# Two MLPs behind an attention: stages spread, fewer loads, and one head group's q and k transposed on VectorE

## The chip, the cores and the metric

The kernel runs on one core of a Trainium2 chip. The metric is device microseconds (us) of one execution; a kernel's time is the median of its runs. Engines are named as the profile names them: PE (TensorE matmuls), PEld (its weight loads), DVE (VectorE), ACT (ScalarE), POOL (GpSimd) and SP (SyncE, which issues nearly all DMAs).

## The reference

Attention over 4 batches, 8 heads, 576 positions of 64 features. Heads 0 to 3 are local (a position sees the 32 before it), heads 4 to 7 strided (a position sees earlier ones that are congruent modulo 32). The output, 2304 tokens of 512, goes through two MLPs (hidden width 2048). The attention weights are float32; the four MLP weight matrices are float64 and are given to the kernel as their 64 bits.

```python
scores = where(mask, scale * (q @ k.T), -1e9)
attn   = softmax(scores)
x = (attn @ v).transpose(0, 2, 1, 3).reshape(2304, 512)
h = x @ w_in;  g = h * clip(h + 3, 0, 6) / 6;          x = g @ w_out      # first MLP
h = x @ w_in2; g = max(h, 0) + log1p(exp(-abs(h)));    out = g @ w_out2   # second MLP
```

## The kernel before

**Tiling.** Layer `l` = 0 is the first MLP, `l` = 1 the second. A layer runs over token chunks `c` and, inside a chunk, over 16 steps `f` of 128 hidden features. Layer 0 has five chunks: `c` = 0 with 384 tokens (the first 96 positions of all four batches) and then one batch per chunk, 480 tokens each. Layer 1 has chunks of 384 and 4 times 512. Every product is made in three passes on a high and a low half of both operands (xh/xl, wih/wil, gh/gl, woh/wol), so step `f` is 12 matmuls into `psh` (`pe_h`, L619) and 12 (layer 1: 9 or 12) into the four banks of `psy` (`pe_y`, L677), the latter two steps late: `psy` of `f` is issued after `psh` of `f` + 2. `psh` has two banks, so `psh` of `f` + 2 waits until the activation of `f` has been read out of its bank.

**The activation** (`post1`): ACT reads `psh` into `r` (L633; in layer 1 three passes, L638 to L640), DVE forms the product (`r` L634, in layer 1 L641) and with that frees the bank. `post2a` casts `r` to `gh` on ACT (L648), `post2b` forms `gl` on DVE (L654).

**Weights.** A tile of 128x512 float64 words (512 KB) is loaded by SP into one of four buffers with the tag `w64` (`load_win` L94, `load_wout` L99). `w_scale` (ACT, L110) and `w_bits` (DVE, L115 and L126) turn it into float32 in place (for w_out into `wor`), and `split_win` (ACT L137, DVE L138) and `split_wout` (ACT L144, DVE L145) make the two halves. A `w64` buffer is free once its last reader on DVE or ACT is through. In chunk 0 of layer 0 one w_in tile and one w_out tile are prepared per step `f`; layer 1's w_in tiles are prepared during the last chunk of layer 0, its w_out tiles during its own chunk 0.

**Attention.** A prologue computes the first 96 positions of every batch. The other 480 positions of batch `b` are worked in slots, two per step, during chunk `c` = `b` of layer 0, and are the input of chunk `b` + 1: stage 0 the strided heads, stage 1 the local ones. `s_load` fetches the strided heads' q, k and v for each of two head pairs (`sq`, `sk`, `vs`); `s_trans` transposes q and k on PE (18 transposes of a batch into `psq`, L462) and copies them out on ACT (`qT`, `kT`, 6 copies, L472). Then scores on PE (`pss`, L489), maximum on DVE (L509), exponentials on ACT (`sc`, L524), `psp` (transposes of the weights, L540), copied by ACT to `pt` (L546), `pso` (times v, L560), division on DVE (`xn`, L570) and `psx` (L586), which becomes xh/xl (L159 and L160). The table at the end of the builder says in which slot each piece is put.

**What sets the order.** The code is written in a framework that fixes each engine's order when the program is built; each engine then works through its list in that order, and an instruction that waits holds all that stand behind it on its engine. `after(...)` makes the pieces in its body be ordered behind a marked instruction ("DVE" is the last `r` of layer 0, "PE" the last matmul of `pe_h`). SP's list holds the DMA issues.

Of the kernel before, what the change touches and what calls it, by code (L numbers as in the profile page):

```python
# [16 lines left out]
P = 128  # L17
# [5 lines left out]
def attn_two_mlps(  # L23
# [68 lines left out]
    def load_win(l, f):  # L92
        t = wsl.tile([P, DM], I64, tag="w64", name="wi64", bufs=4)
        nc.sync.dma_start(out=t, in_=w_in[l][f].rearrange("p k f -> p (k f)"))  # L94
        wst_t[0, l, f] = t

    def load_wout(l, f):
        t = wsl.tile([P, DM], I64, tag="w64", name="wo64", bufs=4)
        nc.sync.dma_start(out=t, in_=w_out[l][f * P : (f + 1) * P, :])  # L99
        wst_t[1, l, f] = t  # L100
# [168 lines left out]
    def loc_c(bp, e):  # L269
        s = loc[bp]["s", e][0]  # L270
        ps = ps_att("psc")
        for i in range(2 * NP):
            nc.tensor.transpose(ps[:KW, i * QB : (i + 1) * QB], s[:, i], ident[:QB, :QB])
        if e == 0:
            loc[bp]["pts"] = ap.tile([P, NP, 512], F32, tag="pt", name="pt")
        pt = loc[bp]["pts"][:, e]
        nc.scalar.copy(pt[:KW, : 2 * NP * QB], ps[:KW, : 2 * NP * QB])
        loc[bp]["pt", e] = pt
# [120 lines left out]
    def s_load(b, pr):  # L399

        q, k = (in_tile(n) for n in ("sq", "sk"))
        rows = slice(b * STRIDE, (b + 1) * STRIDE)
        n = STRIDE // NG
        for g in range(NG):
            for e in range(2):
                nc.sync.dma_start(
                    out=q[:, g * P + e * D : g * P + (e + 1) * D],
                    in_=qs[b * STRIDE + n * g : b * STRIDE + n * (g + 1), 2 * pr + e, II - 1 :, :],
                )
        for g in range(5):  # L410
            r0, r1 = KR * g, min(KR * (g + 1), STRIDE)
            nc.sync.dma_start(
                out=k[: (r1 - r0) * NJ, g * P : (g + 1) * P].rearrange("p (h d) -> p h d", d=D),
                in_=ks[
                    2 * pr : 2 * pr + 2, b * STRIDE + r0 : b * STRIDE + r1
                ].rearrange("h r j d -> (r j) h d"),
            )
# [6 lines left out]
        un[0, b, pr] = dict(q=q, k=k, v=v)  # L424

# [10 lines left out]
    def l_load_v(b, pr):  # L436

        v = v_tile("vl")
        for e in range(2):
            v3 = v[e * D : (e + 1) * D].rearrange("k (i o d) -> k i o d", o=2, d=D)  # L440
            fs = slice((2 * pr + e) * D, (2 * pr + e + 1) * D)
            for o in range(2):
                n = SB // BL // 2 + 1 - o
                k0 = 2 * BL + o * BL
                nc.sync.dma_start(
                    out=v3[:, :n, o],
                    in_=vl[b, k0 : k0 + n * 2 * BL, fs].rearrange("(i k) d -> k i d", k=2 * BL),
                )
        un[1, b, pr]["v"] = v

    def s_trans(b, n, last=False):
# [82 lines left out]
    def a_pt(st, b):  # L534

        ps = ps_two("psp")
        pt = ap.tile([P, NP, 512], F32, tag="pt", name="pt")
# [90 lines left out]
    def post1(l, c, f):  # L628
# [30 lines left out]
    def pe_y(l, c, f):  # L659
# [8 lines left out]
        for m in range(n):  # L668
# [7 lines left out]
            for j, (a, bb) in enumerate(prods):  # L676
                nc.tensor.matmul(  # L677
                    o, lhsT=a, rhs=bb, start=(f == 0 and j == 0), stop=(f == NF - 1 and j == 2)
                )
# [51 lines left out]
    for b in range(B):  # L731
        o = 2 * NF * b + (3 if b == 0 else 0)
# [5 lines left out]
        put(o - 1, s_trans, b, "q")  # L738
        put(o, s_trans, b, "k")
        put(o + 1, s_trans, b, "k", True)  # L740
        for st, qk, exp, rec, pt, pv, px in (
            (0, 3, (5, 6, 7, 8), 9, 10, 12, 15),
            (1, 7, (10, 11, 13, 14), 16, 18, 20, 23),
        ):
            put(o + qk, a_qk, st, b)
            for pr in range(NP):
                put(o + qk + pr, a_max, st, b, pr)
            for n in range(2 * NP):
                put(o + exp[n], a_exp, st, b, *divmod(n, 2))
            put(o + rec, a_rec, st, b)  # L750
            put(o + pt, a_pt, st, b)
            put(o + pv, a_pv, st, b)
            put(o + px, a_px, st, b)

    with ExitStack():
# [113 lines left out]
        for pr in range(NP):  # L869
            s_load(0, pr)  # L870
        with after("xh", "xl"):
            w_scale(1, 0, 0)
# [6 lines left out]
        for n, (l, c, f) in enumerate(seq):  # L879
# [36 lines left out]
            if l == 1 and c == 0:  # L916
                if f == 0:
                    w_bits((0, 1, NF - 1))
                w_bits((1, 1, f))
            if c == 0:  # L920
                split_wout(l, c, f)
            if att:
                for u in fill.get(2 * (NF * c + f), []):
                    with after(*(["DVE", "PE"] if c == 0 else [])):
                        u()
# [5 lines left out]
            if last1:  # L931
                w_scale(0, 1, f)
                if f == NF - 1:
                    w_scale(1, 1, 0)
            if l == 1 and c == 0 and f + 1 < NF:
                w_scale(1, 1, f + 1)
            if att:
                for u in fill.get(2 * (NF * c + f) + 1, []):
                    with after(*(["DVE", "PE"] if c == 0 else [])):
                        u()  # L940
# [71 lines left out]
```

## Time and profile before

| | |
|---|---|
| median of 3 runs | 900.32 us (899.03 to 905.15) |
| profiled execution | 898.38 us, its span 896.2 us |
| mean granted clock | 0.986 of full speed |
| PE busy | 867.1 us (97%) |
| ACT busy | 519.2 us (58%) |
| DVE busy | 458.3 us (51%) |

Some 2.2 us of the profiled execution lie outside the span. PE is busy nearly all the time, so time can only be had where PE does less or where it waits; the other engines' shares are means over stretches that differ much, and have to be read by stretch.

### The profile page before, as it was taken

To read this page: it belongs to the slowest core of one execution; us is meant where nothing else is said; L and a number is where in the kernel's file an instruction comes from. 1 tells how busy PE (TensorE), PEld (TensorE's weight loads), DVE (VectorE), ACT (ScalarE), POOL (GpSimd) and SP (SyncE) were. 2 spreads that over 40 slices of the span, in tenths; PEclk is the share of its full clock that TensorE was granted. 3 is DMA by queue.
4 is the path that set the end of the run, shared out by engine and by line. 5 is a ranking of instruction groups with operands and counts; after the bars stand their busy time and mean duration, and the time that the engine had idled before them with its cause. 6 is when DMAs were issued, how large, how long until landed. Compare 5 with 4: busy or idle time off the path is not lost.

```text
span 896.2 us, 15445 instructions
## 1 busy us (share of the span) xinstructions
PE 867.1 (97%) x6107; PEld 747.6 (83%) x6107; DVE 458.3 (51%) x1019; ACT 519.2 (58%) x1142; POOL 7.6 (1%) x17
## 2 busy tenths in 40 slices
PE   4898899999999999999999899999999999999997
PEld 2797898888888888888888788888888888888996
DVE  6897855443544344455767664433443344334433
ACT  4687657434734375345545876655655565555664
POOL 3000000000000000000000000000000000000000
PEclk8899999999999999999999999999999999999999
DMA  8778831211331032004335620200110001000100
GB/s 241 222 237 200 277 91 45 64 28 29 91 69 27 24 103 47 2 3 125 108 95 194 223 95 15 68 1 0 36 48 1 1 0 48 1 1 9 39 1 36
DMA packets 82504, 65.92 MB, mean 74 GB/s; under 512 B 63872, under 2 KB 70912, under 8 KB 82432
## 3 DMA queue, kind: packets, MB, share of 16 engines
q1 hardware_dynamic: 81424, 64.35, 24.3%
q8 instruction: 48, 0.79, 0.4%
q10 hardware_dynamic: 1008, 0.59, 0.2%
q14 instruction: 24, 0.20, 0.1%
HBM read 55.44 MB, written 9.44 MB: 72 GB/s over the span
## 4 chain that ended last, share of the span: by engine, by line
PE 79%; DMA 9%; DVE 4%; ACT 4%; issue 2%; SPq 1%; ACTq 0%; DVEq 0%
PE psh L619 37%; PE psy L677 37%; DMA wi<-in_w_in_dram 5%; DMA wo<-in_w_out_dram 3%; ACT sc L524 1%; PE pso L560 1%; DVE wil L138 1%; PE pss L489 1%; ACT wi L110 1%; SPq L695 1%; PE psp L540 1%; PE psx L586 1%; ACT wo L110 1%; PE psq L462 1%; DMA lq<-in_ql_dram 1%
## 5 line engine op out<-in xcount | busy, mean ns | idle before, releaser
L619 PE MATMUL psh<-xh,wih 128*128 128x480 f32 (+2 forms) x640 | 238.9, 373 | 4.8 <-DVE r L641 2.5
L619 PE MATMUL psh<-xl,wih 128*128 128x480 f32 (+2 forms) x640 | 237.7, 372 | 0.0
L619 PE MATMUL psh<-xh,wil 128*128 128x480 f32 (+2 forms) x640 | 237.7, 372 | 0.0
L145 DVE TENSOR_TENSOR wol<-wor,woh 128x512 fp32r<-128x512 f32 x160 | 110.3, 690 | 72.1 <-ACT woh L144 68.7
L144 ACT CAST woh<-wor 128x512 fp32r<-128x512 f32 x160 | 99.0, 619 | 75.6 <-PE psy L677 74.1
L619 PEld LDWEIGHTS psh<-xh,wih 128*128 128x128 f32 x640 | 121.0, 189 | 23.4 <-DVE r L641 3.8
L619 PEld LDWEIGHTS psh<-xl,wih 128*128 128x128 f32 x640 | 121.0, 189 | 16.3 <-DVE xl L160 0.4
L641 DVE SCALAR_TENSOR_TENSOR r<-psh,r 128x512 f32<-128x512 f32 (+1 forms) x80 | 51.0, 638 | 161.4 <-ACT r L640 161.4
L619 PEld LDWEIGHTS psh<-xh,wil 128*128 128x128 f32 x640 | 120.9, 189 | 14.8
L654 DVE TENSOR_TENSOR gl<-r,gh 128x480 fp32r<-128x480 f32 (+2 forms) x160 | 101.5, 634 | 45.6 <-ACT gh L648 45.5
L677 PE MATMUL psy<-gl,woh 128*128 128x480 f32 (+1 forms) x320 | 119.9, 375 | 0.5 <-DVE gl L654 0.5
L677 PE MATMUL psy<-gh,wol 128*128 128x480 f32 (+1 forms) x320 | 118.5, 372 | 0.4 <-DVE wol L145 0.4
L677 PE MATMUL psy<-gh,woh 128*128 128x480 f32 (+1 forms) x320 | 118.4, 375 | 0.0
L648 ACT CAST gh<-r 128x480 fp32r<-128x480 f32 (+2 forms) x160 | 92.1, 575 | 42.7 <-DVE r L634 38.4
L677 PE MATMUL psy<-wol,gh 128*128 128x512 f32 x288 | 111.9, 391 | 0.0
L677 PE MATMUL psy<-woh,gl 128*128 128x512 f32 x288 | 111.6, 391 | 0.0
L677 PE MATMUL psy<-woh,gh 128*128 128x512 f32 x288 | 110.9, 390 | 0.0
L638 ACT ACTIVATE r<-psh 128x512 f32<-128x512 f32 (+1 forms) x80 | 44.4, 555 | 93.8 <-PE psh L619 93.6
L634 DVE SCALAR_TENSOR_TENSOR r<-r,psh 128x480 f32<-128x480 f32 (+1 forms) x80 | 50.4, 630 | 80.2 <-ACT r L633 80.1
L633 ACT ACTIVATE r<-psh 128x480 f32<-128x480 f32 (+1 forms) x80 | 44.5, 556 | 61.7 <-PE psh L619 60.3
L677 PEld LDWEIGHTS psy<-gl,woh 128*128 128x128 f32 x320 | 60.4, 189 | 9.0 <-DVE gl L654 1.3
L677 PEld LDWEIGHTS psy<-gh,wol 128*128 128x128 f32 x320 | 60.3, 189 | 8.5 <-DVE wol L145 1.1
(104 smaller groups left out, 834.6 us busy)
## 6 DMA issues: line engine op xcount, KB each, us to landing
wi<-in_w_in_dram SPq DMA_DIRECT2D x32, 512.0 KB
wo<-in_w_out_dram SPq DMA_DIRECT2D x32, 512.0 KB
out_dram<-vout SPq DMA_DIRECT2D x18, 256.0 KB
ydr<-ysb SPq DMA_DIRECT2D x80, 48.0 KB
yr<-ydr SPq DMA_DIRECT2D x16, 192.0 KB
vs<-in_vs_dram SPq DMA_DIRECT2D x16, 144.0 KB
sq<-in_qs_dram SPq DMA_DIRECT2D x64, 32.0 KB
lk<-in_kl_dram SPq DMA_DIRECT2D x8, 256.0 KB
```

Of the source, the lines that this page charges most:

```text
L110: nc.scalar.activation(out=h, in_=h, func=AF.Prelu, scale=2.0**-112, alpha=-(2.0**32))
L138: nc.vector.tensor_tensor(out=lo, in0=raw, in1=hi.bitcast(F32), op=ALU.subtract)
L144: nc.scalar.copy(hi, raw)
L145: nc.vector.tensor_tensor(out=lo, in0=raw, in1=hi.bitcast(F32), op=ALU.subtract)
L619: mark["PE"] = nc.tensor.matmul(ps[:, :n], lhsT=w[:, kt], rhs=x[:, :n], start=(kt == 0 and j == 0), stop=(kt == KT - 1 and j == 2),)
L633: nc.scalar.activation(out=r, in_=ps, func=AF.Relu, bias=3.0)
L634: mark["DVE"] = nc.vector.scalar_tensor_tensor(out=r, in0=r, scalar=6.0, in1=ps, op0=ALU.min, op1=ALU.mult)
L638: nc.scalar.activation(out=r, in_=ps, func=AF.Abs)
L641: nc.vector.scalar_tensor_tensor(out=r, in0=ps, scalar=0.0, in1=r, op0=ALU.max, op1=ALU.add)
L648: nc.scalar.copy(hi, g32_t[l, c, f])
L654: nc.vector.tensor_tensor(out=lo, in0=g32_t.pop((l, c, f)), in1=hi.bitcast(F32), op=ALU.subtract)
L677: nc.tensor.matmul(o, lhsT=a, rhs=bb, start=(f == 0 and j == 0), stop=(f == NF - 1 and j == 2))
```

## The change

- The loaded 512 KB weight tiles get five buffers in place of four.
- For batches 2 to 4 (`b` = 1 to 3) q and k of the strided heads are loaded by 4 + 4 DMAs per head pair, each 32 partitions by 16 or 18 rows of 128 bytes, in place of 8 + 5 DMAs with rows of 256 bytes; a new function `s_trans32` transposes them on DVE, four instructions a batch, and the PE transposes and ACT copies of these batches go. Batch 1 keeps the transposes on PE; its k comes in 3 DMAs per pair in place of 5.
- v of the strided heads is loaded by a function of its own (`s_load_v`), v of the local heads in 2 DMAs per pair in place of 4. SP's list goes from 379 rows to 329.
- The slots of the attention's pieces are spread: the exponentials of stage 1 lie at 14 to 20, its last piece at 28 of 32 (before: 10 to 14 and 23); q and k of batches 3 and 4 are loaded 14 slots ahead.
- In layer 1's chunk 0 the w_out tile is loaded two steps ahead in place of one, its `w_scale` is ordered behind the `gh` cast of the step, its `w_bits` behind the `r` of the step. The pieces of attention are ordered behind the last `psh` matmul in all chunks, and "PE" now marks matmuls of `pe_y` too.

```diff
     def load_win(l, f):
-        t = wsl.tile([P, DM], I64, tag="w64", name="wi64", bufs=4)
+        t = wsl.tile([P, DM], I64, tag="w64", name="wi64", bufs=5)
...
         q, k = (in_tile(n) for n in ("sq", "sk"))
...
+        else:
+            for t, w, src in ((q, NR, qs[rows, :, II - 1 :, :]), (k, NJ, ks[:, rows])):
+                for i in range(4):
+                    h, d0 = 2 * pr + i // 2, i % 2 * BL
+                    nc.sync.dma_start(
+                        out=t[i * BL : (i + 1) * BL, : w * BL].rearrange("r (j d) -> r j d", d=BL),
+                        in_=(src[:, h] if t is q else src[h])[:, :, d0 : d0 + BL],
+                    )
+        un[0, b, pr] = dict(q=q, k=k)
...
+    def s_trans32(b, n, pr):
+        u = un[0, b, pr]
+        w = NR if n == "q" else NJ
+        u[n + "T"] = st_tile(n + "T")
+        nc.vector.transpose(
+            out=u[n + "T"][:, : STRIDE * w].rearrange("p (r j) -> p j r", j=w),
+            in_=u[n][:, : STRIDE * w].rearrange("p (j r) -> p j r", r=STRIDE),
+        )
...
-            nc.vector.scalar_tensor_tensor(
+            mark["DVE2"] = nc.vector.scalar_tensor_tensor(
                 out=r, in0=ps, scalar=0.0, in1=r, op0=ALU.max, op1=ALU.add
             )
...
-        nc.scalar.copy(hi, g32_t[l, c, f])
+        mark["ACT"] = nc.scalar.copy(hi, g32_t[l, c, f])
...
-                put(o - 6, s_load, b, pr)
+                put(o - (14 if b > 1 else 5), s_load, b, pr)
+                put(o - 5, s_load_v, b, pr)
             put(o + 3, l_load_qk, b, pr)
-            put(o + 13, l_load_v, b, pr)
...
-            (0, 3, (5, 6, 7, 8), 9, 10, 12, 15),
-            (1, 7, (10, 11, 13, 14), 16, 18, 20, 23),
+            put(o + 18, l_load_v, b, pr)
...
+            (0, s0 + 4, (8, 9, 11, 13) if b == 1 else (6, 8, 10, 12), 14, 17, 20),
+            (1, o + 9 + (b == 1), (14, 16, 18, 20), 22, 25, 28),
...
-                if f == NF - 1:
-                    load_wout(1, 0)
-            if l == 1 and c == 0 and f + 1 < NF:
-                load_wout(1, f + 1)
+                if f >= NF - 2:
+                    load_wout(1, f - NF + 2)
+            if l == 1 and c == 0 and f + 2 < NF:
+                load_wout(1, f + 2)
...
             if l == 1 and c == 0:
-                if f == 0:
-                    w_bits((0, 1, NF - 1))
-                w_bits((1, 1, f))
+                with after("DVE2"):
+                    if f == 0:
+                        w_bits((0, 1, NF - 1))
+                    w_bits((1, 1, f))
...
             if l == 1 and c == 0 and f + 1 < NF:
-                w_scale(1, 1, f + 1)
+                with after("ACT"):
+                    w_scale(1, 1, f + 1)
```

Pieces of the engines' lists at three stretches of the program, before and after. In them `wi` and `wo` with a number are single weight tiles.

ACT, at the start of chunk 0, from the last copies of the prologue to the first activation `r`, before (`wi_402` and `wo_404` are w_in of step 4 and w_out of step 1):

```order
L159 CAST xh<-psd 128x192
L137 CAST wih<-wi_130 128x512
L110 ACTIVATE wi_337<-wi_337 128x512
L110 ACTIVATE wi_356<-wi_356 128x512
L144 CAST woh<-wor 128x512
L137 CAST wih<-wi_337 128x512
L137 CAST wih<-wi_356 128x512
L633 ACTIVATE r<-psh 128x384
L110 ACTIVATE wi_402<-wi_402 128x512
L110 ACTIVATE wo_404<-wo_404 128x512
```

The same place after (`wi_398` and `wo_400` are these two tiles now, `wi_437` is w_in of step 5):

```order
L110 ACTIVATE wi_398<-wi_398 128x512
L159 CAST xh<-pst 128x3x4x32
L110 ACTIVATE wo_128<-wo_128 128x512
L137 CAST wih<-wi_130 128x512
L159 CAST xh<-psd 128x192
...
L137 CAST wih<-wi_356 128x512
L137 CAST wih<-wi_398 128x512
L110 ACTIVATE wo_400<-wo_400 128x512
L665 ACTIVATE r<-psh 128x384
L110 ACTIVATE wi_437<-wi_437 128x512
```

The scale of step 4's w_in tile has moved from behind the first `r` to ahead of the prologue's last copies, and that of step 1's w_out tile to ahead of the first `r`.

DVE at the same place, from the last differences `xl` of the prologue, after:

```order
L115 TENSOR_SCALAR wi_398<-wi_398 128x512
L160 TENSOR_TENSOR xl<-psd,xh 128x192
L126 SCALAR_TENSOR_TENSOR wi_398<-wi_398 128x512
L160 TENSOR_TENSOR xl<-pst,xh 128x3x4x32
...
L126 SCALAR_TENSOR_TENSOR wor<-wo_128 128x512
...
L115 TENSOR_SCALAR wo_400<-wo_400 128x512
L138 TENSOR_TENSOR wil<-wi_356,wih 128x512
L138 TENSOR_TENSOR wil<-wi_398,wih 128x512
L126 SCALAR_TENSOR_TENSOR wor<-wo_400 128x512
L115 TENSOR_SCALAR wi_437<-wi_437 128x512
L666 SCALAR_TENSOR_TENSOR r<-r,psh 128x384 x2
```

Before, `xl<-psd` and `xl<-pst` followed each other with no weight tile between them, and only the L115 of `wi_402` stood ahead of the first `r`; now three tiles' conversions do.

DVE late in chunk 0, at step 11 or so, after (`qT` and `kT` are the transposed q and k of batch 2):

```order
L115 TENSOR_SCALAR wo_1027<-wo_1027 128x512
L478 STREAM_TRANSPOSE qT<-sq 128x16x32
L138 TENSOR_TENSOR wil<-wi_958,wih 128x512
L478 STREAM_TRANSPOSE kT<-sk 128x18x32
L666 SCALAR_TENSOR_TENSOR r<-r,psh 128x384
```

The transposes of batch 2 stand among chunk 0's weight conversions; those of batches 3 and 4 stand in chunks 1 and 2 or later.

ACT at the change of layers, from the last `gh` of layer 0 on, before:

```order
L110 ACTIVATE wo_5899<-wo_5899 128x512
L648 CAST gh<-r 128x480
L110 ACTIVATE wo_5940<-wo_5940 128x512
L638 ACTIVATE r<-psh 128x384
L639 ACTIVATE r<-r 128x384
L110 ACTIVATE wo_5985<-wo_5985 128x512
L640 ACTIVATE r<-r 128x384
L144 CAST woh<-wor 128x512
L110 ACTIVATE wo_6030<-wo_6030 128x512
L648 CAST gh<-r 128x384
```

And after:

```order
L680 CAST gh<-r 128x480
L110 ACTIVATE wo_5425<-wo_5425 128x512
L144 CAST woh<-wor 128x512
L670 ACTIVATE r<-psh 128x384
L671 ACTIVATE r<-r 128x384
L672 ACTIVATE r<-r 128x384
L680 CAST gh<-r 128x384
L110 ACTIVATE wo_5472<-wo_5472 128x512
```

Before, scales of w_out tiles stood ahead of and between the passes of layer 1's first `r`; now one stands behind each `gh`.

## Rows read from the trace of the kernel before

**Rows 1.** The page, part 1: busy us (share of the span) and instructions of each engine.

```profile
PE 867.1 (97%) x6107; PEld 747.6 (83%) x6107; DVE 458.3 (51%) x1019; ACT 519.2 (58%) x1142; POOL 7.6 (1%) x17
```

**Rows 2.** Busy time by stretch; last three columns: granted clock, DMA share, GB/s.

```profile
45.00:60.00 15.00, 15.00 (x209) 14.55 (x207) 14.01 (x57) 12.11 (x33) 0.00 (x0) 1.00 0.78 269
80.00:98.00 18.00, 17.42 (x99) 16.77 (x98) 15.05 (x30) 11.73 (x21) 0.00 (x0) 0.94 0.94 246
...
37.10:119.50 82.40, 76.26 (x903) 72.58 (x904) 70.09 (x193) 63.27 (x166) 0.00 (x0) 0.96 0.76 230
...
119.50:470.00 350.50, 349.88 (x3142) 302.47 (x3141) 172.58 (x449) 180.37 (x461) 0.00 (x0) 1.00 0.22 59
489.00:522.00 33.00, 29.76 (x137) 25.63 (x136) 24.25 (x47) 25.98 (x53) 0.00 (x0) 0.95 0.75 247
522.00:896.00 374.00, 369.53 (x1694) 313.77 (x1692) 153.28 (x244) 221.49 (x392) 0.00 (x0) 1.00 0.05 18
```

**Rows 3.** Timeline of PE: places where it waited, and one matmul at 80.5.

```profile
37.15 0.44 PE L619 MATMUL psh<-xh,wih 128*128 128x384 f32 x1 [1.25 <-DVE r L634]
...
68.80 1.06 PE L540 MATMUL psp<-ident,sc 128*128 128x128 f32 x8 [0.86 <-DVE nm L509]
...
77.14 1.64 PE L560 MATMUL pso<-vs,pt 36*32 36x64 f32 x128 [2.06 <-ACT pt L546]
...
80.50 0.53 PE L677 MATMUL psy<-gh,woh 128*128 128x384 f32 x1
...
106.39 0.43 PE L560 MATMUL pso<-vl,pt 64*32 64x64 f32 x4 [2.21 <-issue]
...
332.46 0.85 PE L489 MATMUL pss<-lk,lq 64*32 64x64 f32 x64 [0.62 <-DMA lk<-in_kl_dram]
...
498.15 0.44 PE L619 MATMUL psh<-xh,wih 128*128 128x384 f32 x1 [2.29 <-DVE r L641]
```

**Rows 4.** Timeline of PE, the first transposes of batch 4 in chunk 3.

```profile
306.09 1.03 PE L462 MATMUL psq<-ident,sq 128*128 128x128 f32 x8
306.88 0.46 PE L619 MATMUL psh<-xh,wih 128*128 128x480 f32 x1
```

**Rows 5.** Groups by form in chunk 0, DVE: busy time, mean ns of one.

```profile
L654 DVE TENSOR_TENSOR gl<-r,gh 128x384 fp32r<-128x384 f32 x16 | 8.8, 551 | 2.0 <-ACT gh L648 2.0
...
L160 DVE TENSOR_TENSOR xl<-psx,xh 128x480 fp32r<-128x480 f32 x4 | 3.5, 867 | 0.6 <-ACT xh L159 0.6
```

**Rows 6.** Timeline of SP, DMA issues at the start of chunk 0.

```profile
28.24 2.37 SPq L412 DMA_DIRECT2D sk<-in_ks_dram  x5
30.70 0.85 SPq L420 DMA_DIRECT2D vs<-in_vs_dram  x2
32.21 0.36 SPq L94 DMA_DIRECT2D wi<-in_w_in_dram  x1
```

**Rows 7.** Timeline of DVE at the start of chunk 0.

```profile
29.12 0.36 DVE L160 TENSOR_TENSOR xl<-psd,xh 128x192 fp32r<-128x192 f32 x1
...
30.23 0.42 DVE L115 TENSOR_SCALAR wi<-wi 128x512 int32<-128x512 uint32 x1
...
32.10 0.68 DVE L126 SCALAR_TENSOR_TENSOR wor<-wo 128x512 int32<-128x512 int32 x1
...
36.20 0.43 DVE L115 TENSOR_SCALAR wi<-wi 128x512 int32<-128x512 uint32 x1 [0.41 <-DMA wi<-in_w_in_dram]
```

**Rows 8.** Waits of 465 to 530 us: total us, times, longest.

```profile
ACT wo L110 <- DMA wo<-in_w_out_dram: 8.6, 6, 2.5
```

**Rows 9.** Timeline of ACT at layer 1's first activation.

```profile
494.71 0.69 ACT L110 ACTIVATE wo<-wo 128x512 f32<-128x512 f32 x1 [2.52 <-DMA wo<-in_w_out_dram]
495.29 0.48 ACT L638 ACTIVATE r<-psh 128x384 f32<-128x384 f32 x1
```

**Rows 10.** DMA of 145.2 to 160.6 us, batch 3's q and k: packets; share of 16 engines.

```profile
DMA packets 4077, 1.03 MB, mean 67 GB/s; under 512 B 4074, under 2 KB 4074, under 8 KB 4074
...
q1 hardware_dynamic: 4074, 0.99, 28.3%
```

More of the change, by code (lines that the diff above doesn't have):

```diff
@@ L97, in load_wout @@
     def load_wout(l, f):
-        t = wsl.tile([P, DM], I64, tag="w64", name="wo64", bufs=4)
+        t = wsl.tile([P, DM], I64, tag="w64", name="wo64", bufs=5)
         nc.sync.dma_start(out=t, in_=w_out[l][f * P : (f + 1) * P, :])
@@ L274, in loc_c @@
         if e == 0:
-            loc[bp]["pts"] = ap.tile([P, NP, 512], F32, tag="pt", name="pt")
-        pt = loc[bp]["pts"][:, e]
+            if bp:
+                loc[bp]["pts"] = ap.tile([P, NP, NG, 2, D], F32, tag="xn", name="pt", bufs=1)
+            else:
+                loc[bp]["pts"] = ap.tile([P, NP, 512], F32, tag="pt", name="pt", bufs=1)
+        pt = loc[bp]["pts"]
+        if bp:
+            pt = pt.rearrange("p r g e d -> p r (g e d)")
+        pt = pt[:, e]
         nc.scalar.copy(pt[:KW, : 2 * NP * QB], ps[:KW, : 2 * NP * QB])
@@ L402, in s_load, with s_load_v @@
         rows = slice(b * STRIDE, (b + 1) * STRIDE)
[L403 to L404 removed]
+        if b == 0:
+            n = STRIDE // NG
+            for g in range(NG):
+                for e in range(2):
+                    nc.sync.dma_start(
+                        out=q[:, g * P + e * D : g * P + (e + 1) * D],
+                        in_=qs[b * STRIDE + n * g : b * STRIDE + n * (g + 1), 2 * pr + e, II - 1 :, :],
+                    )
+            r0 = b * STRIDE
             for e in range(2):
                 nc.sync.dma_start(
[L407 to L411 removed]
+                    out=k[: KR * NJ].rearrange("p (g h d) -> p g h d", h=2, d=D)[:, :4, e],
+                    in_=ks[2 * pr + e, r0 : r0 + KFULL].rearrange("(g r) j d -> (r j) g d", g=4),
+                )
             nc.sync.dma_start(
[L413 to L416, printed above, removed]
[L417 removed]
+                out=k[: (STRIDE - KFULL) * NJ, 4 * P :].rearrange("p (h d) -> p h d", d=D),
+                in_=ks[2 * pr : 2 * pr + 2, r0 + KFULL : r0 + STRIDE].rearrange("h r j d -> (r j) h d"),
+            )
+        else:
+            for t, w, src in ((q, NR, qs[rows, :, II - 1 :, :]), (k, NJ, ks[:, rows])):
+                for i in range(4):
+                    h, d0 = 2 * pr + i // 2, i % 2 * BL
+                    nc.sync.dma_start(
+                        out=t[i * BL : (i + 1) * BL, : w * BL].rearrange("r (j d) -> r j d", d=BL),
+                        in_=(src[:, h] if t is q else src[h])[:, :, d0 : d0 + BL],
+                    )
+        un[0, b, pr] = dict(q=q, k=k)
+    def s_load_v(b, pr):
+        rows = slice(b * STRIDE, (b + 1) * STRIDE)
         v = v_tile("vs")
@@ L423, in s_load @@
             )
-        un[0, b, pr] = dict(q=q, k=k, v=v)
+        un[0, b, pr]["v"] = v
     def l_load_qk(b, pr):
@@ L439, in l_load_v @@
         for e in range(2):
[L440 to L448, printed above, removed]
-        un[1, b, pr]["v"] = v
+            src = vl[b, 2 * BL : 4 * BL, (2 * pr + e) * D : (2 * pr + e + 1) * D]
+            (row, _), col = src.ap
+            nc.sync.dma_start(
+                out=v[e * D : (e + 1) * D, : SB // BL * D].rearrange("k (m d) -> k m d", d=D),
+                in_=bass.AP(
+                    tensor=src.tensor, offset=src.offset,
+                    ap=[[row, 2 * BL], [BL * row, SB // BL], list(col)],
+                ),
+            )
+        un[1, b, pr]["v"] = v
+    def s_trans32(b, n, pr):
[5 more added lines that the diff above has]
+            in_=u[n][:, : STRIDE * w].rearrange("p (j r) -> p j r", r=STRIDE),
+        )
     def s_trans(b, n, last=False):
@@ L536, in a_pt @@
         ps = ps_two("psp")
-        pt = ap.tile([P, NP, 512], F32, tag="pt", name="pt")
+        pt = ap.tile([P, NP, 512], F32, tag="pt", name="pt", bufs=1)
         for pr in range(NP):
@@ L676, in pe_y @@
             for j, (a, bb) in enumerate(prods):
-                nc.tensor.matmul(
+                mark["PE"] = nc.tensor.matmul(
                     o, lhsT=a, rhs=bb, start=(f == 0 and j == 0), stop=(f == NF - 1 and j == 2)
@@ L870, in attn_two_mlps @@
             s_load(0, pr)
+        for pr in range(NP):
+            s_load_v(0, pr)
         with after("xh", "xl"):
@@ L923, in attn_two_mlps @@
                 for u in fill.get(2 * (NF * c + f), []):
-                    with after(*(["DVE", "PE"] if c == 0 else [])):
+                    with after(*(["DVE", "PE"] if c == 0 else ["PE"])):
                         u()
@@ L933, in attn_two_mlps @@
                 if f == NF - 1:
-                    w_scale(1, 1, 0)
+                    with after("ACT"):
+                        w_scale(1, 1, 0)
             if l == 1 and c == 0 and f + 1 < NF:
-                w_scale(1, 1, f + 1)
+                with after("ACT"):
+                    w_scale(1, 1, f + 1)
             if att:
                 for u in fill.get(2 * (NF * c + f) + 1, []):
-                    with after(*(["DVE", "PE"] if c == 0 else [])):
+                    with after(*(["DVE", "PE"] if c == 0 else ["PE"])):
                         u()
```

20 lines of the change are left out of this document (12 added, 8 removed).

## The prediction

> **What bounds the kernel now.** I read the busy times first: PE 867.1 of 896.2 us [rows 1]. So only two things can shorten the run: PE work that goes away, and the time PE loses to waits or to a lower clock. Then the table by stretch, looking for where PE's busy time is short of the stretch or the clock under 1.00 [rows 2]. Three kinds of stretch show. From 119.5 to 470 PE is busy 349.88 of 350.5 us at clock 1.00: there the kernel is its PE work. From 522 on it is 369.53 of 374 with nothing in it that the change touches. The losses lie in chunk 0 (37.1 to 119.5: idle 82.40 - 76.26 = 6.1 us, and clock 0.96, worth 0.04 x 82.4 = 3.3 us; together 9.4) and at the change of layers (489 to 522: idle 33.00 - 29.76 = 3.2, clock 0.95, worth 1.65; together 4.9). The timeline of PE names the waits there: `psp` and `pso` behind ACT and DVE, `psh` behind `r` [rows 3]. After the wait of 2.06 us a matmul of 384 columns at 80.50 lasts 0.53 us, where the one at 37.15, itself the first after a wait, has 0.44 [rows 3]: the granted clock fell for a while to its lower level, 1.2 in place of 2.4 GHz, and the stretches with the waits of 2.21 and 2.29 us are below 1.00 as well [rows 2]. The reader is to see that DVE is not a spare engine in chunk 0: 70.09 of 82.40 us there, 14.01 of 15 in the piece where PE is full [rows 2].
>
> **Transposes off PE.** Eight transposes take from 306.09 to the next matmul at 306.88: 0.79 us of PE [rows 4]. A batch has 8 + 8 + 2 of them, 18 x 0.79/8 = 1.8 us; the last two are narrower (72 columns), so I take 1.7. Three batches: -5.1 us (bounds -4.7, if the last two cost nothing, and -5.4). All of it is PE time in chunks 1 to 3, where nothing else sets the end, so it comes off in full. Each of these matmuls lasts some 270 ns in the records; counted so, a batch would have 4.9 us, but they overlap, and the start of the next matmul decides. The Trainium skill (TensorE: Matmul & The Clock Gate, Part 4) gives about 275 ns for a transpose inside a kernel; by that figure the sum of this edit would be -14.9 us, and the trace contradicts it as a cost per transpose. The six ACT copies a batch that go too are off the path there (ACT 180.37 of 350.5) [rows 2].
>
> **Transposes on DVE.** No row shows such an instruction. The nearest are other passes of DVE: 384 contiguous elements in 0.55 us, 480 elements written with a stride in 0.87 [rows 5]; scaled to 512 to 576 elements 0.6 to 1.1 us, four a batch: 2.4 to 4.4 us. For batches 3 and 4 DVE has room (172.58 of 350.5 us busy) and this costs nothing unless an `r` stands behind a late load. For batch 2 the order puts them into chunk 0, where they add to DVE's 70.09; I take 3.0.
>
> **Small loads.** q and k of a batch were 4074 packets in 28.3% of 15.4 us, so 15.4 x 0.283 x 16 / 4074 = 17 ns each on one of 16 engines [rows 10]. Half as long a row makes twice as many: another 4.4 us of all 16 engines if a packet costs the same, nothing if it goes by bytes. In chunks 1 to 3 the DMA share is 0.22, so nothing either way. In chunk 0 it falls into 80 to 98 us, with the share at 0.94 [rows 2], and may push weight tiles back: 0 to +4.4, of which I take nothing, since the change issues fewer DMAs there too (16 in place of 26 for q and k of batch 2, at some 0.5 us of SP each: five took 2.37 [rows 6]). The Trainium skill (DMA: Bandwidth & Descriptors, Specifications) wants at least 512 B for line rate and says that smaller ones are read, modified and written; that speaks for the dear end, and by it the sum would be 4.4 us higher. The rows fit with it, but cannot show what 128 B cost.
>
> **The start of chunk 0: a new wait.** The order shows the scale and the conversion of step 4's w_in tile ahead of the prologue's last `xh` and `xl`, which the first matmuls need. When does it land? Before, the last two `vs` were issued by 31.55. The new list has four `sk` and two `vs` less ahead of the tile: 4 x 0.47 + 0.85 = 2.7, so it is issued at about 28.8, and a tile issued at 32.21 let DVE go at 36.20, 4.0 later [rows 6, 7]. So it lands at 32.8, and ACT, DVE and PE stand from 29.1 on: 3.7 us. Then DVE has 2.0 us of conversions and `xl`, 2.55 us from its L115 at 30.23 to the end of its L126 at 32.78 [rows 7], and frees at 37.3 the buffer into which step 1's w_out tile goes; that lands at 41.3, and its L115, two L138, its L126 and another L115 (2.9 us) all stand ahead of the first `r`. So step 2's `psh`, which was at 37.15, starts at about 44.2 (43.4 if the instructions overlap as closely as elsewhere): +7 us. The PE idle before it, some 5 us, is longer than the waits that brought the lower clock: another +1.7.
>
> **The rest of chunk 0.** What then of those +8.7? DVE is ahead by one w_in and one w_out tile (about 2.5 us), against 3.0 more for the transposes. With PE 7 us late, the waits of 0.86 and 2.06 us are covered: ACT reaches `pt` no later than before, as its waits at the start (3.7 us, and some 2.5 for step 1's w_out tile) are about what it idled up to 60 us, of which 15 - 12.11 = 2.9 lie between 45 and 60 alone. If every loss of the stretch went, -9.4, the chunk would end 0.7 earlier than before; if none did, 8.7 later. PE full with DVE at 14.01 of 15 [rows 2] shows that the pace can be had; for it DVE needs some 70.6 of 75 us. I take +1.0, near the good end, and bounds of -5 (a start wait of 3 in place of 7 us, and five buffers) and +7.
>
> **The change of layers.** Here ACT's list held scales of w_out tiles ahead of the passes of the first `r` and between them, and they waited for their transfers: 8.6 us in 6 waits [rows 8]; one scale waited 2.52 us until 494.71, the first pass of `r` stood behind it, and PE waited 2.29 us for that `r` [rows 9, 3]. After, one scale stands behind each `gh`, and its tile was loaded two steps ahead (2 x 21 matmuls at 369.53/1694 = 0.22 us, 9 us of PE work [rows 2], against 4 us for a landing), so nothing late stands ahead of `r`. What is late next is `wol` of the first step, needed two steps after; it has the same slack. -4.9, all the losses of the stretch (bounds -2 and -5.8). One wait of 0.62 us for `lk` in chunk 3 [rows 3] may go with fewer issues ahead of it: -0.4 (0 to -0.8).
>
> **The sum.** -5.1 + 1.0 - 4.9 - 0.4 = -9.4 against the profiled 898.38: 889.0. The median of the runs, 900.32, is 1.9 above the profiled one, so 890.9, and I say 891.
>
> **Rivals.**
> 1. The start wait is never made good: +7 in place of +1.0. DVE's 85% in the chunk speaks for it, the full 45 to 60 against. -3.4: 896.9.
> 2. Five buffers and fewer issues feed chunk 0 better than I allow: -5 in place of +1.0, -15.4 in all: 884.9. For it: 2.06 and 2.21 us waits are single events with a cause that the new slots move; against it: the start wait in the list.
> 3. Slower than before: the wait at step 2 repeats. In chunk 0 each step has two tiles' conversions ahead of an `r` on DVE, and where one lands late PE loses what it lost at 37.15, 1.25 us. On top of +7 (sum -3.4) three more such steps bring the time to 900.7, over the old one; eight of the thirteen left make 906.9. The DMA share of 0.94 from 80 on speaks for it; five buffers, and the fact that such a wait shows once in before, against it.
> 4. The layer change isn't mended: the tiles are late also behind `gh`, and `woh` waits in place of `r`. The term -4.9 falls away: 895.8. Against it stands the slack of 9 us.
>
> **How the numbers follow.** Chances: the forecast 0.44, rival 1 0.18, rival 2 0.22, rival 3 0.06, rival 4 0.10. A measurement of this kernel tells 1% from no change, which is 891.3 and 909.3. The forecast lies at the bound: half of it falls below, rival 2 all below, rivals 1, 4 and most of 3 between: faster 0.47, within 1% 0.49, slower 0.04. The range takes rival 2 (885, less 1 us for the bounds of transposes and layer change) to the upper bounds of rivals 1 and 4 (897 + 2): 884 to 899; what it leaves is rival 3 and ends of rival 2.
>
> **What would show it.** No `psq` in chunks 1 to 3 and PE's busy time 5 us less there; ACT at 29 us waiting 3 to 4 us for a weight tile and step 2's `psh` at 43 to 45; no PE wait over 1 us between 486 and 522 and no clock under 1.00 there; chunk 0 ending between 114 and 126. I am wrong if the tile lands much earlier, if the clock stays low after the early wait for longer than one of the three dips before, or if DVE's transposes take over 1.1 us.

## The result

The changed kernel takes 893.3 us in the median (889.42 to 896.3, 8 runs), the kernel before 901.62 (898.46 to 905.15, 8 runs): a ratio of 0.9912, with a 95% interval of 0.9891 to 0.9932. The prediction was 891 us, 884 to 899. The profiled execution of the changed kernel took 893.29 us, its span 891.5, so 4.7 us less than the span before; that of before (898.38) lay at the fast end of its runs, which is why the medians differ by more than the profiles do.

Three marks on PE's timeline split that: the first `psy` matmul of 480 columns (chunk 0 is through by then; the column "end of chunk 0" further down is this mark), the first `psh` of layer 1 (384 columns), and the first `psh` of layer 1's chunk 1 (512 columns). Columns: start us, us, instruction. Before:

```profile
130.88 0.38 PE L677 MATMUL psy<-gh,woh 128*128 128x480 f32 x1
...
485.06 0.33 PE L619 MATMUL psh<-xh,wih 128*128 128x384 f32 x1
...
559.18 0.39 PE L619 MATMUL psh<-xh,wih 128*128 128x512 f32 x1
```

After:

```profile
136.27 0.38 PE L709 MATMUL psy<-gh,woh 128*128 128x480 f32 x1
...
485.57 0.33 PE L651 MATMUL psh<-xh,wih 128*128 128x384 f32 x1
...
554.58 0.39 PE L651 MATMUL psh<-xh,wih 128*128 128x512 f32 x1
```

Chunk 0 ends 5.4 us later, although 16 of batch 2's 18 transposes lay ahead of the mark before and are gone. From there to layer 1 it takes 349.3 us in place of 354.2, 4.9 less; the change of layers 69.0 in place of 74.1, 5.1 less. So two of the terms came and one went the other way. The table by stretch of the changed kernel (columns as in [rows 2]):

```profile
35.00:45.00 10.00, 7.54 (x24) 6.51 (x25) 8.46 (x18) 7.52 (x14) 0.00 (x0) 0.55 0.47 142
45.00:60.00 15.00, 14.59 (x91) 14.28 (x90) 13.48 (x28) 12.42 (x27) 0.00 (x0) 1.00 0.96 320
...
46.40:126.00 79.60, 74.07 (x900) 70.83 (x901) 72.19 (x195) 61.18 (x162) 0.00 (x0) 0.98 0.86 245
119.50:470.00 350.50, 350.50 (x3128) 303.33 (x3128) 185.31 (x467) 175.99 (x451) 0.00 (x0) 1.00 0.24 57
489.00:522.00 33.00, 32.17 (x163) 29.02 (x162) 23.81 (x45) 26.99 (x54) 0.00 (x0) 1.00 0.65 212
```

The change of layers has lost its idle time (0.8 us left of 3.2) and its low clock. The start of chunk 0 has a new one: between 35 and 45 us the granted clock is 0.55. PE's timeline there, and its waits later in chunk 0 and in layer 1:

```profile
30.96 0.45 PE L651 MATMUL psh<-xh,wih 128*128 128x384 f32 x1
36.92 0.69 PE L651 MATMUL psh<-xl,wih 128*128 128x384 f32 x1 [5.52 <-DVE xl L160]
...
46.38 0.45 PE L651 MATMUL psh<-xh,wih 128*128 128x384 f32 x1 [0.41 <-DVE r L666]
...
79.20 1.06 PE L572 MATMUL psp<-ident,sc 128*128 128x128 f32 x8 [1.40 <-DVE nm L541]
85.48 0.44 PE L651 MATMUL psh<-xh,wih 128*128 128x384 f32 x1 [2.16 <-DVE r L666]
91.93 0.69 PE L651 MATMUL psh<-xh,wih 128*128 128x384 f32 x1 [1.66 <-DVE r L666]
...
514.73 0.96 PE L709 MATMUL psy<-woh,gh 128*128 128x512 f32 x3 [0.82 <-ACT woh L144]
```

PE waits 5.52 us for one `xl`; the matmuls after it last 0.52 to 0.69 us until 43.5 us, in place of 0.33 to 0.45, and step 2's `psh`, at 37.15 before [rows 3], starts at 46.38. SP's and DVE's lists show why. SP:

```profile
29.20 0.85 SPq L442 DMA_DIRECT2D vs<-in_vs_dram  x2
30.14 0.40 SPq L94 DMA_DIRECT2D wi<-in_w_in_dram  x1
...
39.75 0.35 SPq L99 DMA_DIRECT2D wo<-in_w_out_dram  x1
```

DVE, at the same place and at the two later waits:

```profile
36.18 0.43 DVE L115 TENSOR_SCALAR wi<-wi 128x512 int32<-128x512 uint32 x1 [5.73 <-DMA wi<-in_w_in_dram]
36.52 0.35 DVE L160 TENSOR_TENSOR xl<-psd,xh 128x192 fp32r<-128x192 f32 x1
...
43.29 0.44 DVE L115 TENSOR_SCALAR wo<-wo 128x512 int32<-128x512 uint32 x1 [0.29 <-DMA wo<-in_w_out_dram]
...
45.78 0.55 DVE L666 SCALAR_TENSOR_TENSOR r<-r,psh 128x384 f32<-128x384 f32 x1
...
82.29 1.07 DVE L478 STREAM_TRANSPOSE qT<-sq 128x512 f32<-128x512 f32 x1
83.21 0.68 DVE L138 TENSOR_TENSOR wil<-wi,wih 128x512 fp32r<-128x512 f32 x1
83.80 1.25 DVE L478 STREAM_TRANSPOSE kT<-sk 128x576 f32<-128x576 f32 x1
84.88 0.55 DVE L666 SCALAR_TENSOR_TENSOR r<-r,psh 128x384 f32<-128x384 f32 x1
...
90.98 0.43 DVE L115 TENSOR_SCALAR wi<-wi 128x512 int32<-128x512 uint32 x1 [1.13 <-DMA wi<-in_w_in_dram]
91.33 0.55 DVE L666 SCALAR_TENSOR_TENSOR r<-r,psh 128x384 f32<-128x384 f32 x1
```

The tile of step 4 is issued at 30.14, DVE and all behind it stand until 36.18. At 84.88 the `r` that PE waits for stands behind two transposes, at 91.33 behind a late weight tile.

### The profile page after: what moved, and what is told of

Same layout as the page of the kernel before. It is cut to its first block, busy times and chain, and to the rows that moved or that the text cites. A ratio compares the mean times of both kernels' runs of the same rounds, so it can differ in the third digit from the quotient of the medians.

```text
span 891.5 us, 15287 instructions
## 1 busy us (share of the span) xinstructions
PE 861.7 (97%) x6053; PEld 743.5 (83%) x6053; DVE 470.1 (53%) x1031; ACT 510.8 (57%) x1124; POOL 7.6 (1%) x17
## 4 chain that ended last, share of the span: by engine, by line
PE 88%; DMA 5%; DVE 4%; ACT 2%; SPq 1%; issue 1%; ACTq 0%; DVEq 0%
PE psy L709 42%; PE psh L651 42%; DMA wi<-in_w_in_dram 2%; PE pso L592 1%; DMA wo<-in_w_out_dram 1%; PE pss L521 1%; PE psx L618 1%; DMA sk<-in_ks_dram 1%; PE psp L572 1%; DVE wil L138 0%; ACT sc L556 0%; DMA yr<-ydr 0%; PE psc L384 0%; DVE wi L126 0%; DVE wor L126 0%
## 5 line engine op out<-in xcount | busy, mean ns | idle before, releaser
L709 PE MATMUL psy<-gl,woh 128*128 128x480 f32 (+1 forms) x320 | 118.0, 370 | 0.0
L709 PE MATMUL psy<-woh,gh 128*128 128x512 f32 x288 | 107.0, 390 | 0.8 <-ACT woh L144 0.8
```

The costliest lines, as they stand in the source:

```text
L709: mark["PE"] = nc.tensor.matmul(o, lhsT=a, rhs=bb, start=(f == 0 and j == 0), stop=(f == NF - 1 and j == 2))
```

## The experiments

The theory to test (A): chunk 0 loses by the early wait for step 4's tile. Against it (B): chunk 0 is set by the work of DVE and ACT and by DMA, and the early wait is made good. From the second group on: what chunk 0 loses besides is DVE's transposes (A2), or the transfers, that is small rows and the weight tiles that land behind them (D). The table has each run's median, its ratio to the kernel before on the same chip with its interval, and from its profile the first `psy` of 480 columns (end of chunk 0), the time from there to layer 1, and from there to layer 1's chunk 1.

| kernel | median us | ratio to before | end of chunk 0 | to layer 1 | change of layers |
|---|---|---|---|---|---|
| before | 901.62 | 1 | 130.88 | 354.18 | 74.12 |
| changed | 893.3 | 0.9912 (0.9891 to 0.9932) | 136.27 | 349.30 | 69.01 |
| tile behind xh, xl | 891.7 | 0.9907 (0.9888 to 0.9927) | 131.84 | 349.20 | 69.78 |
| + early load | 887.63 | 0.9865 (0.9848 to 0.9883) | 132.14 | 349.15 | 69.43 |
| four buffers | 891.61 | 0.9913 (0.9892 to 0.9934) | 133.09 | 349.26 | 69.88 |
| before + DVE transposes | 899.34 | 0.9985 (0.9970 to 0.9999) | 135.40 | 348.78 | 72.03 |
| early load + late transposes | 884.83 | 0.9805 (0.9773 to 0.9837) | 126.80 | 349.19 | 69.16 |
| early load, transposes twice | 893.47 | 0.9901 (0.9870 to 0.9932) | 136.04 | 349.13 | 69.62 |
| early load, batch 2 on PE | 892.29 | 0.9885 (0.9852 to 0.9918) | 132.59 | 348.97 | 72.33 |
| before + change of layers | 895.42 | 0.9920 (0.9888 to 0.9951) | 131.54 | 353.83 | 68.10 |
| early + late + late casts | 884.18 | 0.9826 (0.9803 to 0.9849) | 129.43 | 349.13 | 67.92 |
| changed + late transposes | 894.46 | 0.9944 (0.9922 to 0.9966) | 136.34 | 349.12 | 71.73 |
| changed, again | 892.32 | 0.9914 (0.9894 to 0.9933) | 135.30 | 349.15 | 69.46 |
| early + late, rows twice | 890.25 | 0.9890 (0.9869 to 0.9912) | 133.15 | 349.26 | 69.54 |

The marks come from one execution each, and executions with the same order differ. The changed kernel has 136.27 and 135.30; the kernel before and the one with the change of layers alone have the same order up to the last chunk of layer 0 (130.88 and 131.54), and so have the two runs with early load and late transposes (126.80 and 129.43). So a single difference below some 2.6 us in chunk 0 is not read. The change of layers varies as much: 74.12 and 72.03 for before and before + DVE transposes, which have the same order there, and 69.01 to 72.33 for the changed kernel and its variants without the late casts. The ratios rest on 4 to 17 runs of either kernel; the median before lay between 899.6 and 901.9 us from group to group, so ratios and medians can differ by 2 us or so, and both are given where they do.

**The tile of step 4 ordered behind the prologue's last xh and xl.**

```diff
-                with after(*(["xh", "xl"] if f == 0 else [])):
+                with after(*(["xh", "xl"] if f < 2 else [])):
                     w_scale(0, 0, f + 3)
```

> The changed kernel with the scale and conversion of step 4's w_in tile ordered behind the prologue's last xh and xl; everything else as changed. Theory A (the early wait for this tile is what chunk 0 loses): the 5.5 us wait of PE for xl and the 10 us at the lower clock go, step 2's psh starts at 38 to 42 in place of 46 us, chunk 0 ends 5 to 7 us earlier, the median comes to 886 to 889. Theory B (chunk 0 is set by the work of DVE and ACT and by DMA, the early wait is idle time that they make good anyway): the wait moves to a later place, chunk 0 ends within 2 us of the changed kernel's, median 892 to 895.

Chunk 0 ended 4.4 us earlier in the profile, but the profiled execution (889.53) was the fastest of five and the ratio is that of the changed kernel within the interval. In its trace one `xl` still stands behind an L115 that waited for its tile until 34.14, and PE waited 2.50 us for it. So the order alone moves the wait by one row and makes it shorter; the medians show no gain. The expectation of A (886 to 889) was missed by some 3 us.

**And the tile loaded ahead of batch 1's q, k and v.**

```diff
         load_win(0, 3)
+        load_win(0, 4)
         for pr in range(NP):
             s_load(0, pr)
...
-                if f + 4 < NF:
+                if 0 < f < NF - 4:
                     load_win(0, f + 4)
```

> As the run before, and step 4's w_in tile is loaded ahead of the q, k and v loads of batch 1 rather than behind them, so that it has landed long before it is scaled. Theory A: no engine waits for it at all, step 2's psh starts at 37 to 40 us, chunk 0 ends 6 to 8 us earlier than in the changed kernel, median 885 to 888. Theory B: as in the run before, 892 to 895. If the late loads of batch 1 take over as the wait, psq waits for q near 36 us instead.

887.63 us, 0.0047 or 4.2 us below the changed kernel by the ratios, and 4.1 us earlier at the end of chunk 0 (3.2 against the changed kernel's second profile). PE's timeline:

```profile
31.63 0.45 PE L651 MATMUL psh<-xl,wih 128*128 128x384 f32 x1 [0.24 <-DVE xl L160]
38.03 0.45 PE L651 MATMUL psh<-xh,wih 128*128 128x384 f32 x1 [2.13 <-DVE r L666]
...
69.38 1.94 PE L572 MATMUL psp<-ident,sc 128*128 128x128 f32 x8 [3.34 <-DVE nm L541]
```

Step 2 starts 8.4 us earlier than in the changed kernel; half of that or more is lost again by the end of the chunk, the largest piece at `psp` (3.34 us). So A holds for some 4 us, and B for the rest.

**Four buffers.**

```diff
-        t = wsl.tile([P, DM], I64, tag="w64", name="wi64", bufs=5)
+        t = wsl.tile([P, DM], I64, tag="w64", name="wi64", bufs=4)
```

(in `load_wout` as well)

> The changed kernel with four weight buffers in place of five. Theory A: the fifth buffer is what let the tile be brought forward, so without it the early wait goes: step 2's psh at 37 to 39 us, median 886 to 890, faster than the change as it is. Theory B (five buffers feed chunk 0 and the change of layers): waits for weight tiles come back in chunk 0 or at the change of layers, median 894 to 898.

The list at the start is that of before again, so it is the fifth buffer that let the tile come forward. But the time is that of the changed kernel. DVE and PE at the place where it is lost:

```profile
82.10 1.26 DVE L478 STREAM_TRANSPOSE kT<-sk 128x576 f32<-128x576 f32 x1 [1.66 <-DMA sk<-in_ks_dram]
83.20 0.68 DVE L138 TENSOR_TENSOR wil<-wi,wih 128x512 fp32r<-128x512 f32 x1
83.81 0.53 DVE L686 TENSOR_TENSOR gl<-r,gh 128x384 fp32r<-128x384 f32 x1
```

```profile
84.39 0.69 PE L709 MATMUL psy<-gl,woh 128*128 128x384 f32 x1 [4.67 <-DVE gl L686]
```

A transpose waits for its `sk`, and `gl` stands behind it. Neither theory had this; the change of layers didn't need the fifth buffer.

**The kernel before with the DVE transposes alone** (their loads and `s_trans32` as in the change's diff, in the slots of before).

> The kernel before with one part of the change: q and k of batches 2 to 4 loaded in 32-partition pieces and transposed on DVE, the slots, buffers and all else as before. Theory A (the transposes cost PE 1.7 us a batch and some 0.3 for each change between them and other matmuls, and DVE hides its own): chunks 1 to 3 lose 5 to 6.5 us, chunk 0 within 1.5 us of before, median 894 to 897. Theory C (DVE's transposes and the 128 B rows of batch 2 cost chunk 0 what they save later): chunk 0 ends 3 to 5 us later, median 899 to 901.

899.34 us, a gain of 0.15%: theory C. In the profile, an execution of 894.88 us and the fastest of twelve, chunk 0 ends 4.5 us later, and to layer 1 it takes 5.4 us less. At 84.91 PE waits 5.55 us for a `gl` that stands on DVE behind the conversion of a w_out tile. That tile was issued at 78.25 and landed at 83.96; before, a tile issued at 77.89 was as slow, until 84.30, but no `gl` that PE waited for stood behind it. So in this trace the order on DVE made the wait, not a slower transfer.

**Batch 2's transposes kept out of chunk 0** (with the early load).

```diff
+        with after(*(["DVE"] if b == 1 else [])):
             nc.vector.transpose(
```

> As the run with the early load, and batch 2's four transposes are ordered behind chunk 1's second r, so that chunk 0's DVE has none of them (4.7 us by the rows of the changed kernel: 1.07 for q, 1.26 for k, twice); the loads stay. Theory A2 (what chunk 0 still loses, some 2.9 us, is DVE's transposes in a full engine): chunk 0 ends 2 to 4 us earlier than in the run with the early load, median 884 to 886.5. Theory D (it is the small rows and the weight tiles that land late behind them): chunk 0 ends within 1 us of that run, median 887 to 889.

884.83 us. By the ratios it is 0.0060 less than with the early load alone, 5.4 us; by the medians 2.8, since the kernel before ran at 901.88 us beside this run and at 900.24 beside the other. Chunk 0 ends 5.3 us earlier, 2.7 in the second profile of this order. So A2 holds, with 3 to 5 us.

**The same transposes issued twice** (with the early load, in chunk 0).

```diff
+        for _ in range(2 if b == 1 else 1):
             nc.vector.transpose(
```

> As the run with the early load, with batch 2's transposes issued twice each into the same tiles: 4.7 us more of DVE in chunk 0. Theory A2: chunk 0 ends 3 to 5 us later, median 890 to 893. Theory D: within 1.5 us, median 887 to 889.

3.9 us later at the end of chunk 0, 3.2 us by the ratios and 5.8 by the medians, for 4.6 us of DVE. A2 again.

**Batch 2 on the old path** (with the early load): 256 B rows and PE transposes for `b` = 1.

```diff
-        if b == 0:
+        if b <= 1:
             n = STRIDE // NG
...
-        if b == 0:
+        if b <= 1:
             for n, a in enumerate((("q",), ("k",), ("k", True))):
```

> As the run with the early load, with batch 2 left on the old path: 256 B rows, 18 PE transposes in chunk 1, only batches 3 and 4 on DVE. Theory A2 and D alike let chunk 0 end 2 to 3 us earlier and chunk 1 take 1.7 to 2 longer, median 886.5 to 888; if chunk 0 does not gain, the new path of batch 2 costs it nothing and the median comes to 889 to 890.

892.29 us, a miss; by the ratios the run can't be told from the early load alone (0.9885 and 0.9865, with intervals that overlap). The mark of chunk 0 lies 0.45 later, with some 1.9 us of transposes ahead of it, so chunk 0 itself gained about 1.4, less than two profiles of one order differ. The change of layers is 2.9 us longer, though its order is that of the run with the early load: PE waits there for `woh`, and on ACT casts of the next chunk's tokens, which wait for their loads, stand ahead of it. PE, then ACT:

```profile
512.77 1.65 PE L709 MATMUL psy<-woh,gh 128*128 128x512 f32 x3 [2.54 <-ACT woh L144]
```

```profile
509.27 0.62 ACT L159 CAST xh<-yr 128x512 fp32r<-128x512 f32 x1 [1.73 <-DMA yr<-ydr]
```

The changed kernel has the same wait with 0.82 us, and 1.30 in its second profile. So the run doesn't tell what the new path of batch 2 costs chunk 0.

**The kernel before with the change of layers alone** (loads two steps ahead, scales behind `gh`, conversions behind `r`, as in the change's diff).

> The kernel before with one part of the change: w_out of layer 1 loaded two steps ahead, its scales behind gh and its conversions behind r; four buffers, all else as before. If the stall at the change of layers is the order of ACT's scales, it goes as a whole: 4 to 5.5 us less between the first psh of layer 1 and its chunk 1, median 895 to 896.5. If it needs the fifth buffer, 2 us less at most, median 898 to 900.

895.42 us, 0.8% less than before, 7 us by the ratio (interval 4 to 10); the profile has 6.0 us less at the change of layers and nothing elsewhere. The earlier loads and the new order do it together, with four buffers; which of the two does how much was not separated. The wait for `woh` doesn't come in this run.

**Early load, late transposes, and the casts of layer 1's next tokens behind `gh`.**

```diff
-                split_y(c + 1 if l == 1 else 0, f - 6)
+                with after(*(["ACT"] if l == 1 and c == 0 else [])):
+                    split_y(c + 1 if l == 1 else 0, f - 6)
```

> The early load and the late transposes of batch 2, and in layer 1's chunk 0 the casts of the next chunk's tokens (xh from yr) ordered behind the gh cast of their own step, so that ACT does not stand on their loads ahead of woh. If the wait of psy for woh near 505 us (1.2 to 2.7 us of PE in all runs with the new layer change and the early slots) is these casts, it goes: 1 to 2 us faster than the run with late transposes, ratio to the kernel before 0.978 to 0.980. If the wait stays or moves behind chunk 0 of layer 1, no difference: 0.980 to 0.982.

The wait is gone, PE is full there (table by stretch):

```profile
484.00:517.00 33.00, 33.00 (x168) 29.96 (x167) 22.47 (x42) 25.82 (x53) 0.00 (x0) 1.00 0.61 198
```

and the change of layers is 1.2 us shorter. The times can't tell it from the run without: 884.18 against 884.83 us, with intervals that overlap. In this profile chunk 0, whose order is the same, ended 2.6 us later.

**Late transposes without the early load.**

> The changed kernel with the late transposes of batch 2 alone; the early wait for step 4's tile stays. If the two losses of chunk 0 add up, the wait near 31 us is as in the changed kernel, chunk 0 ends 4 to 6 us earlier than there, and the ratio to before is 0.985 to 0.987. If the early wait only hid behind the transposes, 0.990.

0.9944, no faster than the changed kernel on the same chip (0.9914; the medians are 894.46 and 892.32). The early wait is there (5.68 us), and chunk 0 gained nothing (136.34): the two losses don't add. What the profile is slower by lies at the change of layers, 2.3 to 2.7 us, where the wait for `woh` has 1.79. In chunk 0, DVE, then PE:

```profile
89.59 0.43 DVE L115 TENSOR_SCALAR wi<-wi 128x512 int32<-128x512 uint32 x1 [2.95 <-DMA wi<-in_w_in_dram]
89.93 0.55 DVE L687 TENSOR_TENSOR gl<-r,gh 128x384 fp32r<-128x384 f32 x1
```

```profile
90.54 0.69 PE L710 MATMUL psy<-gl,woh 128*128 128x384 f32 x1 [5.21 <-DVE gl L687]
```

Now a weight tile that lands late stands ahead of `gl`. A2 alone can't be the whole cause.

**The changed kernel again.**

> The changed kernel again, on the same chip as the two others, as their measure: ratio to before 0.989 to 0.993 by every theory; the profile shows whether the early wait and the wait for woh come in every execution: the first at 30 to 36 us with 5 to 6 us, the second at 510 to 515 with 0.8 to 2.5.

892.32 us, the same ratio. PE's early wait was there with 6.89 us, that for `woh` with 1.30.

**The 128 B loads of batch 2 issued twice** (with early load and late transposes), the second time into DRAM that nothing reads.

```diff
+                    if b == 1:
+                        z = dram.tile([BL, w * BL], F32, name=f"z{pr}{w}{i}")
+                        with after("ld"):
+                            nc.sync.dma_start(out=z.rearrange("r (j d) -> r j d", d=BL), in_=...)
```

> As the run with early load and late transposes, and each 128 B load of batch 2's q and k is issued a second time behind the first, into a scratch buffer in DRAM that nothing reads: 16 more DMAs on SP, 8704 more packets in chunk 0. Theory D (in the second half of chunk 0 it is DMA and SP that set when weight tiles land, and DVE waits for them ahead of r and gl): chunk 0 ends 3 us or more later, ratio to before 0.984 to 0.992. Theory A2 (DVE's own work there sets it, DMA has room): within 1.5 us of the run with late transposes, ratio 0.979 to 0.983.

0.9890 against 0.9805, 7.6 us slower (5.4 by the medians), and 6.4 us at the end of chunk 0, 3.7 against the second profile of the order without: theory D. Between 37 and 133 us DVE waited 12.0 us for weight tiles, against 6.6 and 9.4 in those two. DMA from 60 to 98 us, with the rows twice:

```profile
DMA packets 18254, 8.44 MB, mean 222 GB/s; under 512 B 16831, under 2 KB 16831, under 8 KB 18249
...
q1 hardware_dynamic: 18249, 8.38, 93.0%
```

and without:

```profile
DMA packets 14888, 9.52 MB, mean 250 GB/s; under 512 B 13088, under 2 KB 13088, under 8 KB 14883
...
q1 hardware_dynamic: 14883, 9.45, 97.1%
```

and without in the run with the late casts as well, which has the same order in chunk 0:

```profile
DMA packets 14623, 8.57 MB, mean 225 GB/s; under 512 B 13055, under 2 KB 13055, under 8 KB 14618
...
q1 hardware_dynamic: 14618, 8.50, 96.9%
```

The DMA engines are nearly full in all three. The bytes moved by 98 us don't show the price, since the two runs without the second rows differ by as much as the run with them does from the first. The run also had a longer wait at step 2, 3.02 us in place of 1.53 and 2.17, and it has 16 more issues on SP; what the packets cost by themselves was not separated from the issues.

## Why the prediction was right or wrong

The direction and the range held, and the median was 2.3 us above the one predicted. One term of the sum was wrong by more than 6 us. The time is nearer to the prediction than that since the other terms came out 1.4 us larger, and by luck: profile against profile the change gave 5.1 us of the 9.4 forecast, median against median 8.3, since the profiled execution before was a fast one. Two of the three signs of being wrong that the prediction named came: the clock stayed low for some 10 us, longer than in any dip before, and one of DVE's transposes takes over 1.1 us.

- **Transposes off PE, -5.1.** Right, too small. From chunk 0's mark to layer 1 it takes 4.9 us less, of which 0.62 is the wait for `lk` and 0.2 the last two transposes of batch 2: 2.0 us for each of two batches in place of 1.7. Three batches: -6.1. The rows of before have most of the difference, beside the transposes themselves: the first `psh` behind them starts at 306.88 [rows 4] and the next one at 307.18, 0.30 later, where two others lie 0.22 apart. The trace speaks against counting each transpose with the 270 ns of its record, which would have been 4.9 a batch.
- **Change of layers, -4.9 and -0.4 for `lk`.** Right: -5.1 and about -0.6, and -6.0 by itself, each to some 2 us, since 72.03 was measured with the old order as well as 74.12. What I named as late next was `wol`; it was `woh`, by casts of the next chunk's tokens that stand ahead of it (0.82 us, up to 2.5); behind `gh` they cost nothing. Rival 4's mechanism is there with a small price.
- **The start of chunk 0.** The mechanism was right, with each step longer. The tile was issued at 30.14 in place of 28.8, 1.3 of which is a prologue that came late by as much (`xl<-psc` at 28.61 and 29.89); it landed 6.0 us later in place of 4.0. From 30.1 to 36.2 us the DMA engines moved 1.14 MB with 2485 packets under 512 B; before, from 32.2 to 36.2, as much (1.16 MB) with 1074 such packets. PE lost 5.5 us in place of 3.7, and the clock stayed at its lower level for most of the 10 us from 35 on, which I had put at 1.7 us of loss. From 31 to 131 us the granted clock was 0.93 (0.90 in the second profile) in place of 0.97. Step 2 came at 46.38 in place of 44.2.
- **The rest of chunk 0, +1.0 in the sum.** This step failed. Chunk 0 ended 5.4 us later with 1.9 us of transposes less ahead of the mark: +7.3 in place of +1.0, about rival 1's +7. (Rival 1's whole time, 896.9, was not reached, as the other terms came out larger.) I had let the early wait be hidden since ACT would reach `pt` no later, and had taken the end near to PE's pace. But the later waits of before were replaced by others that stand behind DVE: `nm` at 79.20, `r` at 85.48 and 91.93, the last behind a late tile, which is rival 3's mechanism. With the early load some 4 us come back.
- **Transposes on DVE, 3.0 in chunk 0.** Over the upper bound: 1.07 and 1.25 us, 4.6 a batch. With the early load, moving them out of chunk 0 is worth 3 to 5 us, and doubled they cost another 3 to 6. Without it their place makes no gain (0.9944). So their price depends on what else stands in DVE's list.
- **Small rows, taken as nothing.** The bounds held, the value taken from them didn't. The rows under this list give 10.6 x 0.588 x 16 / 7776 = 12.8 ns for a row of 128 B, against 17 ns for one of 256 B, counted as in the prediction (batch 4's, from 246.2 to 257.2, have 12.9). So half the row costs three quarters of the time, and a batch with its 8704 rows costs all 16 engines 7.0 us in place of 4.6: 2.3 more, in the middle of the bounds of 0 to 4.4. In chunk 0, where they were at 0.94 [rows 2], 8704 more packets with their issues cost 4 to 6 us. An engine moves 15 bytes per ns with rows of 256 B and 10 with rows of 128. The Trainium skill's rule (DMA: Bandwidth & Descriptors, Specifications), that transfers under 512 B miss line rate, agrees with these numbers, which fall with the row.

Batch 3's q and k in the changed kernel, from 154.2 to 164.8 us, with no other load beside them:

```profile
DMA packets 7778, 1.00 MB, mean 94 GB/s; under 512 B 7776, under 2 KB 7776, under 8 KB 7776
...
q1 hardware_dynamic: 7776, 0.97, 58.8%
```

What stays open: how much of chunk 0's loss in the second half is DVE's work and how much late transfers. Either, when doubled, costs PE about what it takes (4.6 us of DVE, 7.0 us of the DMA engines); each run has another instruction that waits for a landing ahead of `r` or `gl`, and I have not separated the two. The best kernel here, early load and late transposes, is 0.9805 of the one before (0.9826 with the late casts), about 1% faster than the change as it stands.

## What to carry to other kernels

An extra buffer lets a scheduler bring a load's consumer forward, and on an engine that works in order the consumer then holds whatever stands behind it: look in the new order for every instruction that waits for a transfer, and ask when that transfer is issued. In a stretch where PE, DVE, ACT and the DMA engines are all busy for three quarters of the time or more, take no wait as hidden by another and no small piece of work as free. Work taken off the engine that bounds is a gain in stretches where the engine that takes it over has room (here chunks 1 to 3), and may be a loss in the one where it hasn't.

## What the runs showed of the hardware

A transpose in 32x32 blocks on DVE took 1.07 us for 128x512 and 1.25 for 128x576 float32, 2.1 to 2.2 ns for each element of a partition, against 1.35 in a contiguous pass (0.69 us for 512). Its output is written with a stride; whether the stride or the transpose makes the difference was not measured.

After the wait that ended at 36.92 us the granted clock was 0.55 on average from 35 to 45 us: matmuls of 384 columns lasted 0.52 to 0.69 us until 43.5 us, 6.6 us after the wait was over, with PE at work in between.

A row of 128 B from DRAM took 12.8 to 12.9 ns of one of the 16 DMA engines in two quiet stretches, one of 256 B 17 ns.
